# Strassen for two thirds of the first batch element's up projections, and its softmax denominators from one term

## The chip, the cores and the metric

The kernel runs on one core of a Trainium2 chip. A core has five engines that run their own instruction streams: TensorE for matmuls (PE in the profile, its weight loads are PEld), VectorE (DVE), ScalarE (ACT), GpSimd (POOL) and SyncE (SP), which issues most of the DMA transfers here. The metric is the device time of one execution in microseconds; the number given for a kernel is the median of several runs.

## The reference, cut to what matters

Routing attention is followed by a bilinear feed-forward block. Queries and keys are each assigned to the nearest of 16 centroids, and a query sees only the keys of its own cluster.

```python
# attention: batch 4, heads 8, sequence 768, head size 64
mask = q_assign[:, :, :, None] == k_assign[:, :, None, :]
scores = scale * np.matmul(q, k.transpose(0, 1, 3, 2))
scores = np.where(mask, scores, -1000000000.0)
scores = scores - np.max(scores, axis=-1, keepdims=True)
attn = np.exp(scores)
attn = attn / (np.sum(attn, axis=-1, keepdims=True) + 1e-09)
out = np.matmul(attn, v)
# feed-forward: x is (3072, 512), w_a and w_b (512, 1536), w_out (1536, 512)
a = x @ w_a
b = x @ w_b
y = (a * b) @ w_out
```

The weights arrive as 64-bit floats, so the kernel rounds them to 32 bits itself. Everything is computed in float32.

## The kernel before: the parts that the change touches

The program works in **groups**. There are 16 pairs of heads (4 batch elements with 4 pairs each), and 6 groups for each pair, 96 in all. A pair has two halves of 384 queries (`hf`), and a half has six tiles of 128 keys (`j`); a group handles two key tiles. In each group TensorE computes scores of the new tiles (`score`), ScalarE their exponentials (`pt`), and TensorE the weighted sums of values of the tiles before (`weigh`). In the time that is left in a group, pieces of the feed-forward block of the batch element before are run from a queue (`ffn`); a credit of columns per group (`PER_GROUP`) spreads them. What remains in the queue after the last group runs alone.

**Sums over the keys.** The exponentials of a half's tiles are added up elementwise, and a matmul with ones sums the result over the 128 partitions. For the first batch element (`p < HP`, that is pairs 0 to 3) VectorE adds the first five tiles, and the sixth goes into the matmul as a term of its own. For the others both engines share the additions.

```python
    def add_up(u):
        p, hf, j = where(u)
        if j == 0 or j == NJ - 1 and p < HP:
            return
        ...
        for a in range(2):
            many = p >= HP and (a == 1 or j in (2, 4))
            eng = nc.gpsimd if many else nc.vector
            eng.tensor_tensor(out=acc[:, a, :],
                in0=probs[u - 1][:, a, :] if j == 1 else acc[:, a, :],
                in1=probs[u][:, a, :], op=ALU.add)

    def denominators(p, hf):
        ps = apart()
        acc = accs.pop((p, hf))
        terms = [acc]
        if p < HP:
            terms.insert(0, probs[p * UPP + hf * NJ + NJ - 1])
        for n, t in enumerate(terms):
            for a in range(2):
                nc.tensor.matmul(out=ps[a * D:(a + 1) * D, 0:HB], lhsT=ones,
                                 rhs=t[:, a, :], start=(n == 0),
                                 stop=(n == len(terms) - 1))
        ... # ScalarE copies the sums out; VectorE inverts; GpSimd scales xT
```

**Up projections.** A tile of weights has 128 columns; each matmul is issued for 64 of them at a time (`in_halves`). For the first batch element `a` and `b` are computed plainly, 384 tokens (`HB`) at a time, with four chunks of the contraction (`NCH`):

```python
    def ffn_block(b, blk):                       # b = 0 only
        def up(w_sb, f):
            ps = in_turn()                       # one of three banks of PSUM
            for ch in range(NCH):
                in_halves(ps[:, 0:HB], w_sb[:, ch, f * P:(f + 1) * P],
                          xTs[b][:, ch, t0:t0 + HB], ...)
            return ps
        def piece_a(f):                          # ScalarE: ha = a
            ...
        def piece_b(f):                          # VectorE: h = ha * b
            ...
```

For the other three batch elements they go by Strassen's method in Winograd's form (`ffn_ups`): for each pair of weight tiles `i`, `i + N2` and for each of `w_a` and `w_b` there are seven products of two chunks each in place of eight. VectorE makes combinations of the weights (S1 to S4) and of the tokens (T1 to T4), ScalarE copies partial results from PSUM, VectorE adds the others to them, and GpSimd multiplies finished halves of `a` and `b`.

```python
    def combine_x(b):              # queued two pieces before the ups of b
        for c in range(2):
            for out, l, r in ((t3, x22, x12), (x12, x12, x11), (t2, x22, x12)):
                nc.vector.tensor_tensor(out=out, in0=l, in1=r, op=ALU.subtract)
    def ffn_ups(b, h):
        def products(w_sb, i, is_a):
            ...                    # half_1: S1, S2; half_2: S3, S4
            return half_1, half_2, [p1, p2, p6, p5, p7, p3, p4]
        parts = [products(w_sb, i, w_sb is wa_sb) for i in range(NF // 2)
                 for w_sb in (wa_sb, wb_sb)]
```

The down projections (`ffn_downs`) go by Strassen for all four batch elements.

**Rounding the weights.** 36 parts of 128 x 512 weights are loaded and rounded by four VectorE instructions and one addition on GpSimd. ScalarE takes the size of the upper word, and one more VectorE instruction (`flush_w`) sets weights that are too small for a float32 to zero:

```python
            nc.vector.scalar_tensor_tensor(out=w, in0=size, scalar=SMALLEST,
                                           in1=w, op0=ALU.is_ge, op1=ALU.mult)
```

**When things are due.**

```python
    EARLY = BG + 1                           # BG = 24, groups per batch element
    for i in range(8, len(w_parts)):
        due.setdefault(23 + int((i - 8) / 1.5), []).append(i)
    keep_busy(12)                            # transposes of nothing, at the start
    ...
        late = int(g > EARLY)
        if g % 3 == late and 0 < g - late:
            denominators(*divmod(g // 3 - 1, 2))
        ...
        first, second = (4, 1) if g <= EARLY else (5, 3 if g < NG else 2)
```

`long_path` is a second program in the kernel that runs only if a check at the end finds values out of range.

## Time and profile before

| | |
|---|---|
| time, median of 3 | 1047.72 us (1047.59 to 1048.28) |
| span of the profiled execution | 1045.6 us, of 1047.88 us |
| PE busy | 1032.8 us, 7163 instructions |
| DVE, ACT, POOL busy | 657.2, 303.1, 329.9 us |
| stage of batch element 0's attention alone | to about 109 us |
| ups of batch element 0, beside attention of 1 | 109.6 us to about 309 us |
| first product of its downs | 309.4 us |
| feed-forward alone at the end | from about 850 us |

The engines run side by side, so their busy times don't add up. A group of instructions in the profile is named by line, engine, operation, and tiles (output, arrow, inputs), followed by a count, busy time and mean duration. "Idle before" is how long the engine stood still just ahead of these instructions, and the arrow behind it names what ended most of that. The time of PE is best read from the distance between starts, since a matmul's record also covers the time in which it passes through the array.

### The profile page before, as it was taken

How to read it: one execution, taken by the hardware profiler on the slowest of the kernel's cores; microseconds unless marked ns; L12 is line 12 of the kernel's file. 1: busy time of each engine (PE TensorE's matmuls, PEld its weight loads, DVE VectorE, ACT ScalarE, POOL GpSimd, SP SyncE). 2: the span in 40 equal slices, each digit the busy share in tenths (PEclk: the TensorE clock that was granted, in tenths of full speed). 3: DMA queues.
4: the chain of work that ended last, by engine and by line, in shares of the span. 5: the costliest groups of instructions: out<-in, count | busy, mean ns of one | idle time of the engine just before them, and what ended most of it. 6: DMA issues, size and time to landing. Idle time of an engine off the chain costs nothing.

```text
span 1045.6 us, 17833 instructions
## 1 busy us (share of the span) xinstructions
PE 1032.8 (99%) x7163; PEld 502.6 (48%) x7163; DVE 657.2 (63%) x1314; ACT 303.1 (29%) x590; POOL 329.9 (32%) x311
## 2 busy tenths in 40 slices
PE   9999999999999999999999999999999999999997
PEld 5444444444445554444444555444444565444564
DVE  6778877887857447555556746765454845554652
ACT  5665333233322222333323122333232201111100
POOL 1111345455543322343442422443333310211100
PEclk9999999999999999999999999999999999999999
DMA  7334343526120121203020030300000000000001
GB/s 183 87 86 86 85 106 105 125 68 144 63 49 20 40 43 23 38 5 46 4 46 3 24 66 22 49 1 20 1 4 1 11 31 21 1 1 1 2 30 34
DMA packets 120521, 46.48 MB, mean 44 GB/s; under 512 B 106608, under 2 KB 115824, under 8 KB 120432
## 3 DMA queue, kind: packets, MB, share of 16 engines
q1 hardware_dynamic: 120016, 44.85, 18.8%
q8 instruction: 58, 0.95, 0.4%
q10 hardware_dynamic: 416, 0.43, 0.1%
q14 instruction: 31, 0.25, 0.1%
HBM read 37.78 MB, written 6.29 MB: 42 GB/s over the span
## 4 chain that ended last, share of the span: by engine, by line
PE 93%; DVE 4%; issue 1%; POOL 1%; ACT 0%; DMA 0%; DVEq 0%; POOLq 0%
PE m L678 62%; PE s L556 15%; PE O L597 12%; PE s L620 1%; PE s L373 1%; PE m L620 1%; DVE raw L755 1%; PE m L373 0%; POOL xT L652 0%; DVE xT L755 0%; DMA h<-in_q_dram 0%; PE m L354 0%; DVE comb L782 0%; DVE acc L586 0%; DVE acc L647 0%
## 5 line engine op out<-in xcount | busy, mean ns | idle before, releaser
L565 ACT ACTIVATE pt<-s 128x768 f32<-128x768 f32 x192 | 145.3, 808 | 206.5 <-PE s L556 161.7
L586 POOL TENSOR_TENSOR acc<-acc,pt 128x384 f32<-128x384 f32 x144 | 152.6, 1073 | 60.2 <-ACT pt L565 43.0
L597 PE MATMUL O<-pt,v 128*64 128x384 f32 x768 | 145.0, 499 | 0.0
L556 PE MATMUL s<-qkT 64*128 64x384 f32 x768 | 139.7, 482 | 0.0
L821 POOL TENSOR_TENSOR h<-h,ha 128x384 f32<-128x384 f32 x54 | 55.5, 1030 | 258.6 <-DVE ha L815 257.7
L678 PE MATMUL m<-xT,wa_sb 128*64 128x384 f32 x672 | 117.5, 487 | 2.7 <-DVE ha L815 1.0
L678 PE MATMUL m<-xT,wb_sb 128*64 128x384 f32 x672 | 116.9, 487 | 0.0
L815 DVE TENSOR_TENSOR ha<-ha,m 128x384 f32<-128x384 f32 x72 | 39.6, 550 | 98.0 <-PE m L678 75.4
L586 DVE TENSOR_TENSOR acc<-acc,pt 128x384 f32<-128x384 f32 x96 | 74.5, 802 | 36.6 <-POOL acc L586 35.5
L815 DVE TENSOR_TENSOR h<-h,m 128x384 f32<-128x384 f32 x72 | 39.5, 548 | 80.7 <-PE m L678 53.8
L812 ACT COPY h<-m 128x384 f32<-128x384 f32 x72 | 34.5, 479 | 184.9 <-PE m L678 184.9
L597 PEld LDWEIGHTS O<-pt,v 128*64 128x64 f32 x768 | 46.6, 136 | 85.8 <-issue 80.1
L678 PE MATMUL m<-wo_sb,h 128*64 128x256 f32 x768 | 86.7, 379 | 0.0
L556 PEld LDWEIGHTS s<-qkT 64*128 64x128 f32 x768 | 70.5, 187 | 31.3 <-issue 0.2
L678 PEld LDWEIGHTS m<-xT,wa_sb 128*64 128x64 f32 x672 | 48.7, 137 | 63.4 <-issue 53.3
L678 PE MATMUL m<-raw 128*64 128x384 f32 x432 | 78.9, 486 | 0.0
L652 POOL TENSOR_TENSOR xT<-xT,acc 128x384 f32<-128x384 f32 x32 | 32.8, 1026 | 144.9 <-DVE acc L647 144.6
L678 PEld LDWEIGHTS m<-xT,wb_sb 128*64 128x64 f32 x672 | 49.0, 137 | 60.1 <-issue 56.2
L678 PEld LDWEIGHTS m<-wo_sb,h 128*64 128x64 f32 x768 | 54.9, 137 | 31.1 <-issue 5.0
L678 PE MATMUL m<-xT,h 128*64 128x256 f32 x576 | 64.5, 379 | 0.0
L678 PE MATMUL m<-xT,size 128*64 128x384 f32 x288 | 52.7, 487 | 0.0
L678 PEld LDWEIGHTS m<-xT,h 128*64 128x64 f32 x576 | 41.3, 137 | 22.3 <-issue 2.3
(169 smaller groups left out, 1302.0 us busy)
## 6 DMA issues: line engine op xcount, KB each, us to landing
raw<-in_moe_w_a_dram SPq DMA_DIRECT2D x12, 512.0 KB, 3.8
raw<-in_moe_w_b_dram SPq DMA_DIRECT2D x12, 512.0 KB, 3.6
raw<-in_moe_w_out_dram SPq DMA_DIRECT2D x12, 512.0 KB, 3.7
qk<-in_q_dram SPq DMA_DIRECT2D x48, 96.0 KB, 3.1
qk<-in_k_dram SPq DMA_DIRECT2D x48, 96.0 KB, 3.6
v<-in_v_dram SPq DMA_DIRECT2D x24, 192.0 KB, 3.8
out_dram<-rest SPq DMA_DIRECT2D x24, 128.0 KB, 1.7
v<-in_v_dram SPq DMA_DIRECT2D x4, 384.0 KB, 4.5
```

Of the source, the lines that this page charges most:

```text
L373: nc.tensor.matmul(out=ps[32 * kq:32 * kq + 32, 0:HB], lhsT=cTb[:, hp, :], rhs=qkTs[p][:, kq * HB:(kq + 1) * HB], start=True, stop=True)
L556: nc.tensor.matmul(out=s[:, a, 0:HB], lhsT=Ts[p][r, S + j * P:S + (j + 1) * P], rhs=Ts[p][r, hf * HB:(hf + 1) * HB], start=start, stop=not ...
L565: nc.scalar.activation(out=pt, in_=s[:, :, 0:HB], func=AF.Exp, scale=SCALE)
L586: eng.tensor_tensor(out=acc[:, a, :], in0=probs[u - 1][:, a, :] if j == 1 else acc[:, a, :], in1=probs[u][:, a, :], op=ALU.add)
L597: nc.tensor.matmul(out=O_of[0][a * D:(a + 1) * D, 0:HB], lhsT=vs[p][:, a, j, :], rhs=probs[u][:, a, :], start=(j == 0), stop=(j == NJ - 1))
L620: nc.tensor.matmul(out=ps[a * D:(a + 1) * D, 0:HB], lhsT=ones, rhs=t[:, a, :], start=(n == 0), stop=(n == len(terms) - 1))
L652: nc.gpsimd.tensor_tensor(out=x, in0=x, in1=den, op=ALU.mult)
L678: nc.tensor.matmul(out=ps[half], lhsT=lhsT[:, half], rhs=rhs, **kw)
L755: nc.vector.tensor_tensor(out=out, in0=l, in1=r, op=ALU.subtract)
L812: nc.scalar.copy(out=box[name], in_=box["X"][:, 0:HB])
L815: nc.vector.tensor_tensor(out=box[name], in0=box[name], in1=box[bank][:, 0:HB], op=ALU.add)
L821: nc.gpsimd.tensor_tensor(out=to, in0=to, in1=box[name], op=ALU.mult)
```

## The change

The change does five things, with the aim of taking matmuls off TensorE and work off VectorE.

1. Of the first batch element's up projections, the weight tiles 0 to 7 (of 12) go by Strassen, in four pairs (0, 2), (1, 3), (4, 6), (5, 7), since the weights of the first tiles are rounded first; tiles 8 to 11 stay plain. Combinations of tokens are made early, and kept in rows of `h` that the plain tiles fill later.
2. In the first batch element the sixth key tile is added up by GpSimd, and the matmul with ones has one term. It comes a group later, and so does the normalization. In the other batch elements GpSimd takes tiles 4 and 5 in place of 2 and 4.
3. The instruction that zeroes small weights is gone. ScalarE looks for a weight that is too small (`see_w`), and if there is one, `long_path` zeroes such weights and computes everything again.
4. The feed-forward block of the first batch element becomes ready as a whole, no longer in two halves, and parts 8 to 35 of the weights come up to three groups later.
5. Smaller moves: the combinations of tokens for batch elements 1 to 3 come in two pieces, fewer empty transposes at the start, and other engines for the first copies.

```diff
 # cuts are marked by ...
     def add_up(u):
-        if j == 0 or j == NJ - 1 and p < HP:
+        if j == 0:
             return
-            many = p >= HP and (a == 1 or j in (2, 4))
+            many = a == 1 or j > 3 if p >= HP else j == NJ - 1
     def denominators(p, hf):
-        terms = [acc]
-        if p < HP:
-            terms.insert(0, probs[p * UPP + hf * NJ + NJ - 1])
-        for n, t in enumerate(terms):
-            for a in range(2):
-                nc.tensor.matmul(... rhs=t[:, a, :], start=(n == 0), ...)
+        for a in range(2):
+            nc.tensor.matmul(... rhs=acc[:, a, :], start=True, stop=True)
...
-        late = int(g > EARLY)
-        if g % 3 == late and 0 < g - late:
+        if g % 3 == 1 and g > 1:
             denominators(*divmod(g // 3 - 1, 2))
-        first, second = 4, 1          # for g <= EARLY
+        first, second = (5, 2) if g <= EARLY else (5, 3 if g < NG else 2)
-    EARLY = BG + 1
+    EARLY = BG + 2
...
     def ffn_ups(b, h):
+        N2, firsts = (NF // 2, range(NF // 2)) if b else (2, (0, 1, 4, 5))
-        parts = [products(...) for i in range(NF // 2) for w_sb in (wa_sb, wb_sb)]
+        parts = [products(...) for i in firsts for w_sb in (wa_sb, wb_sb)]
     def ffn_ready(p, hf):
-        elif hf == 0:
-            blocks[0] = ffn_block(0, 0)
-            ffn.extend(blocks[0][0][0:8])
...
+            for name in ("T3", "T2", "T4"):
+                combination_x(0, name, 1)
+            ffn.extend(ups_first + plain_ups(0, h, range(NF - 4, NF)))
+    def early_steps():
+        return {HP * GPP - 10: both(begin, T("T1", 0)), HP * GPP - 8: T("T1", 1),
+                HP * GPP - 3: T("T3", 0), HP * GPP - 2: T("T2", 0),
+                HP * GPP - 1: T("T4", 0),
+                HP * GPP: lambda: [f() for f in combinations[0:2]],
+                HP * GPP + 1: lambda: combinations[2]()}
...
-            ffn.insert(len(ffn) - FREE_ROOM, (0, lambda: combine_x(b)))
+            for c in range(2):
+                ffn.insert(len(ffn) - FREE_ROOM + c, (0, lambda c=c: combine_x(b, c)))
...
     def round_w(i):
-        size = sizep.tile([P, WN], FP32, name="size")
-        nc.scalar.activation(out=size, in_=halves(FP32)[:, :, 1], func=AF.Abs)
-    def flush_w():
-            nc.vector.scalar_tensor_tensor(out=w, in0=size, scalar=SMALLEST,
-                                           in1=w, op0=ALU.is_ge, op1=ALU.mult)
+    def see_w():
+        while unseen:
+            i, upper = unseen.pop()
+            nc.scalar.activation(out=size, in_=upper, func=AF.Abs)
+            nc.scalar.activation(out=size, in_=size, func=AF.Relu, scale=-STEEP,
+                                 bias=edge[:, 0:1], accum_out=stat[:, n:n + 1])
+            load_w(i + 2)
...
         if p == HP:
-            return [[lambda: across(0), lambda: across(1)], [sims_across],
-                    assign[:2], assign[2:], [one_hot, one_hot_across], []]
+            return [[lambda: across(0), lambda: across(1)],
+                    [sims_across] + assign[:2], assign[2:] + [one_hot],
+                    [one_hot_across], [], []]
-            ready[1] = both(lambda: prep_sim(p), lambda: load_v(p), ready[1])
+            ready[1] = both(lambda: prep_sim(p), lambda: load_v(p), steps[1][0],
+                            lambda: todo.extend(steps[1][1:]))
...
-        due.setdefault(23 + int((i - 8) / 1.5), []).append(i)
+        due.setdefault(26 + int((i - 8) / 1.45), []).append(i)
-        (UP + DOWN * 7 / 8, BG + 5.8), ...
+        (UP * 11 / 12 + DOWN * 7 / 8, BG + 1.8), ...
-    keep_busy(12)
+    keep_busy(5)
     prep_transpose(0, 0)
+    keep_busy(2)
-        if p == 0 and i == 2:
-            nc.vector.tensor_copy(out=dst[:, 0:256], in_=ps[:, 0:256])
-            nc.scalar.copy(out=dst[:, 256:], in_=ps[:, 256:])
-        elif p == 0 and i != 1 or p == 1 and i == 2:
+        if p < 2 and i == 2:
             nc.vector.tensor_copy(out=dst, in_=ps)
```

## The prediction

> **What bounds the kernel now.** I read the page from the top: busy times, then the chain that ended last, then the waits of PE alone, and only then single stretches of the trace.
>
> ```profile
> PE 1032.8 (99%) x7163; PEld 502.6 (48%) x7163; DVE 657.2 (63%) x1314; ACT 303.1 (29%) x590; POOL 329.9 (32%) x311
> PE 93%; DVE 4%; issue 1%; POOL 1%; ACT 0%; DMA 0%; DVEq 0%; POOLq 0%
> PE m L678 62%; PE s L556 15%; PE O L597 12%; PE s L620 1%; PE s L373 1%; PE m L620 1%; DVE raw L755 1%; PE m L373 0%; POOL xT L652 0%; DVE xT L755 0%; DMA h<-in_q_dram 0%; PE m L354 0%; DVE comb L782 0%; DVE acc L586 0%; DVE acc L647 0%
> ```
>
> The first line says that TensorE is nearly always busy and no other engine is above 63%. The second and third say that the chain which sets the end is PE's own work, 62% of it the feed-forward matmuls (L678). A busy PE can still be a slow PE, so I looked at what it waits for. This is the list of waits of PE, whole but for its smallest entries:
>
> ```profile
> PE O L1053 <- DVE ones L80: 1.1, 1, 1.1
> PE m L678 <- DVE ha L815: 1.0, 2, 0.5
> PE s L556 <- DVE sim L481: 1.0, 1, 1.0
> PE m L678 <- POOL xT L652: 0.9, 1, 0.9
> PE m L678 <- DVE rest L939: 0.9, 2, 0.4
> PE m L373 <- DVE cTb L325: 0.6, 1, 0.6
> PE s L620 <- DVE acc L586: 0.5, 1, 0.5
> ```
>
> Columns: total us, times, longest. Added up, PE waits 6 us in a kernel of 1047.72. So time can come almost only from PE work that is not issued, and can go almost only into new waits of PE.
>
> The chain in order of time gives the price of PE work (start, us, what, records):
>
> ```profile
> 152.71 1.44 PE O L597 x8
> 154.16 5.16 PE m L678 x32
> 159.31 1.72 PE s L556 x12
> 161.04 1.44 PE O L597 x8
> ```
>
> 32 records of a feed-forward matmul over 384 tokens take 5.16 us, so one takes 161.2 ns. The groups list 672 such records of xT with wa_sb, while the program issues 336 matmuls of that kind (192 plain ones, 144 of Strassen's products): each matmul in the code leaves two records and costs **322.5 ns**. The mean of 487 ns that the list prints is the passage through the array, three records deep, and is not the price.
>
> **What the Trainium skill says.** (1) "Perfetto Trace Analysis", section "Identifying the Most-Contended Engine": matmul busy share is a poor measure, since pipelined matmuls overlap. The trace agrees (487 ns printed against 161.2 ns of pitch), and that is why I price by pitch. (2) "SBUF — State Buffer", section "SBUF: two separate sides": a VectorE instruction with two SBUF inputs and a GpSimd one exclude each other, each for a whole instruction. The trace fits: VectorE's adds of `acc` and `pt` take 802 ns in the mean, one that begins at 399.58 takes 550, and one at 500.62 takes 1160 while GpSimd adds. Work given to GpSimd therefore slows VectorE. (3) "ScalarE: Activation LUTs", section "Table sets: the hidden batching unit": relu and abs are in every table set. So the new Relu should load no table; before there are two loads, both at the start, of 1283 ns. Were it otherwise, 36 parts would bring up to 72 loads. (4) "TensorE: Matmul & The Clock Gate", section "What's actually happening": the clock falls after an idle window of about 3.4 us. Fewer empty transposes leave gaps of under 1 us at the start, which is far from that; the granted clock in the page never drops below 0.9.
>
> **The change part by part.**
>
> *Up projections.* Plain, the first batch element takes 2 weights x 12 tiles x 2 token blocks x 4 chunks x 2 halves = 384 matmuls. After it, 4 pairs x 2 weights x 7 products x 4 = 224 by Strassen and 4 tiles x 2 blocks x 2 weights x 8 = 128 plain, 352 in all. 32 fewer x 322.5 ns = **10.3 us**, all of it on PE in a stage that PE bounds.
>
> *Denominators.* 8 halves of the first batch element each lose the term of the sixth tile: 2 matmuls each, 16 x 322.5 ns = **5.2 us**. Is PE the bound there too, with no feed-forward work to fill in? Yes: from 14.3 to 98.7 us, the stage of attention alone, it is busy for 83.85 of 84.40 us, and in its timeline a group's matmuls follow on the last one's without a gap. GpSimd pays 16 additions of about 1.07 us; it is busy for only 15.56 us of that stage.
>
> *Start.* The first empty transposes run from 3.84 to 5.94 us, while the copies of the queries that the first real transposes need were done at 5.05. With 5 in place of 12 they can start some 0.5 us earlier. Also, now ScalarE and VectorE each evacuate a part of the last transposes one after the other (7.88 and 8.34 us); VectorE alone will do it at once. The chain through VectorE's cTb (0.6 us wait above) stays. I count **0.5 us**.
>
> *VectorE.* Two stretches show how much room it has (stretch, its length, then busy us and instructions of PE, PEld, DVE, ACT, POOL):
>
> ```profile
> 124.00:310.00 186.00, 185.05 (x1163) 81.41 (x1161) 141.89 (x220) 63.19 (x118) 93.94 (x81) 1.00 0.39 97
> 395.00:565.00 170.00, 169.07 (x1064) 72.70 (x1062) 98.07 (x214) 52.57 (x102) 64.40 (x63) 1.00 0.16 25
> ```
>
> The first is plain ups of batch element 0 together with the rounding: VectorE 76%. The second is Strassen's ups of batch element 1: VectorE 58%. In the first the change takes away the zeroing (27 instructions in this stretch, 28.8 us) and 16 of 24 multiplications at 546 ns (8.7 us). It adds 64 weight combinations at a mean of 376 ns (24.1 us: eight per product set, 288 of them in the kernel before take 108 us), 32 additions at 550 ns and 4 multiplications at 540 ns (19.8 us). Net +6.4 us, in a stage shorter by 10.3 us but for new waits: 148 of some 177 us, **84%**. That is high, but off PE's path as long as the three PSUM banks come free in time. Something helps: in this stretch VectorE stands still for 17.0 us in `acc` additions that wait for GpSimd's (tiles 2 and 4 go to GpSimd in turn with VectorE's 3 and 5). With VectorE doing 1 to 3 and GpSimd 4 and 5, this ping-pong ends.
>
> *ScalarE.* 36 times an Abs (as before, 683 ns) and a Relu with its accumulator read (683 + about 200 ns, from the rows of such reads): +32 us on an engine with 29%. Hidden.
>
> *Waits that move.* The 0.95 us wait of scores for the copy of `sim` at 137.61 should go, as that transpose now follows its matmul directly:
>
> ```profile
> 136.32 0.34 PE L556 MATMUL s<-ohT 64*128 64x384 bf16 x2
> 137.61 0.34 PE L556 MATMUL s<-ohT 64*128 64x384 bf16 x2 [0.95 <-DVE sim L481]
> ```
>
> At 396.4 and 645.3 PE waits 0.43 us each for a bank (the L939 entry), behind six combinations of tokens in a row on VectorE, 5.7 us; cut in two pieces, most of it goes. Together **1.7 us** off. The 0.88 us wait at the first feed-forward piece, for normalized xT, changes form: now the first product that needs the last half is p6, the third, behind three more VectorE subtractions. I leave it as it is.
>
> *New waits.* Strassen beside rounding at 84% VectorE, and the start of it in groups 26 to 28, where normalization, combinations and rounding meet: I allow **1.5 us**. This is a judgement: the ups of batch element 1 show 0.43 and 0.50 us of PE waits, at 58% VectorE; here VectorE is fuller, so I take half as much again.
>
> Sum: -10.3 - 5.2 - 0.5 - 1.7 + 1.5 = -16.2, so 1047.7 - 16.2 = **1031.5 us**, 1.5% less.
>
> **The rivals.**
>
> *VectorE becomes the bound of the first batch element's feed-forward.* For it: 84% busy, in-order work, bursts of four rounding instructions (2.2 us) ahead of an addition that frees a bank, and 12 more GpSimd multiplications that lock the shared port. Against it: at 76%, with 17 us of blocking besides, it costs PE 0.1 us in 20 us. If it wins, 5 to 10 us of the 15.5 come back: 1036 to 1041.
>
> *The denominators wait for GpSimd.* The sum now ends with two GpSimd additions in place of a VectorE one. For it: PE stands in order behind it, 8 times. Against it: the matmul is a group later (3.5 us here at least), GpSimd is nearly idle, 2 x 1.07 us fit. If 0.5 us were lost each time, 4 us come back: 1035.
>
> *The feed-forward starts later and PE starves.* It becomes ready after group 26 and not after 22. But no stretch before has PE idle, so its pieces do not fill holes; they only move to later groups, and what is left runs at the end. It costs nothing unless the bare groups 22 to 26 are bound by VectorE, which is busy for 21.39 of the 25.30 us from 98.7 to 124. I give this 1 to 2 us, inside the range.
>
> *Nothing is gained, for the time was hidden.* PE's 99% and its 6 us of waits speak against it.
>
> **Range and chances.** Both large terms are counts times a measured pitch, so they can hardly be off by 1 us. The uncertain part is waits: at best none are new and the start gains 1 us, 1028.5; at worst VectorE gives back 5 us, 1036.5. Faster by over 2% would need 1026.8 or less, 5 us more than the sum, and there is hardly that much waiting to remove. Slower by over 2% would need 37 us of new waits, such as table loads or the second program running.
>
> **What would show it.** PE records: 7163 - 64 - 32 - 5 = 7062 (an empty transpose leaves one record). In the chain 32 records still take 5.16 us. The L620 groups on `pt` are gone and PE waits for `acc` stay under 1 us in all. VectorE is at 80 to 87% in the ups of batch element 0, its wait for GpSimd's `acc` falls from 35.5 us to under 10. Two table loads. The prediction is wrong if PE's waits add up to more than 10 us, if the pitch changes, or if the first stage of attention shortens by less than 4 us.

## The result, and the profile after

The changed kernel takes **1061.89 us** (median of 4 runs, 1061.72 to 1062.65), the one before 1047.70. The ratio is 1.0136, with a 95% interval of 1.0118 to 1.0153: 1.4% slower, where 1.5% faster had been foreseen. The profiled execution spans 1059.9 us (before 1045.6).

From the page of the kernel after, the busy times and the chain by engine:

```profile
PE 1024.4 (97%) x7062; PEld 493.9 (47%) x7062; DVE 699.2 (66%) x1370; ACT 336.7 (32%) x674; POOL 368.1 (35%) x339
PE 82%; DVE 13%; issue 2%; ACT 1%; POOL 1%; DMA 0%; DVEq 0%; POOLq 0%
```

PE has 7062 records, exactly the number foreseen, so the matmuls did go. But PE is at 97% and no longer 99%, and its share of the chain fell from 93% to 82%, while VectorE's rose from 4% to 13%. VectorE is busy for 42.0 us more and GpSimd for 38.2 us more. The list of PE's waits says where it stands (total us, times, longest):

```profile
PE m L680 <- DVE h L835: 8.2, 5, 3.0
PE m L680 <- ACT h L831: 7.3, 1, 7.3
PE s L563 <- ACT pt L572: 2.9, 8, 0.6
PE m L623 <- POOL acc L594: 2.7, 7, 0.4
PE O L605 <- ACT xT L615: 2.2, 3, 1.2
PE m L680 <- DVE ha L835: 1.9, 2, 1.2
```

The whole list adds up to some 29 us, and before to some 7. Three of these rows (L835 and L831, 17.4 us) are Strassen products that wait for a bank of PSUM or for an operand. The other three (7.8 us) belong to attention: scores wait for the exponentials' buffers, the denominators for the sums, the values for the copies of their results.

Four stretches of the kernel after: attention alone, the groups of the hand-over, its worst piece, and the ups of batch element 0. The columns are the stretch, its length, busy us and instructions of PE, PEld, DVE, ACT and POOL, then the granted clock, the DMA share and GB/s:

```profile
13.50:101.00 87.50, 82.33 (x546) 36.62 (x547) 77.88 (x121) 58.32 (x108) 30.02 (x24) 1.00 0.35 80
101.00:131.00 30.00, 26.75 (x158) 10.61 (x160) 29.45 (x52) 16.28 (x30) 14.28 (x12) 1.00 0.47 95
131.00:150.00 19.00, 10.88 (x60) 4.11 (x58) 17.41 (x26) 4.75 (x12) 11.64 (x10) 0.82 0.31 88
150.00:320.00 170.00, 160.41 (x990) 67.55 (x988) 143.75 (x238) 78.37 (x160) 89.07 (x77) 0.99 0.37 91
```

The last three of the kernel before, for comparison:

```profile
101.00:131.00 30.00, 28.66 (x174) 13.93 (x170) 25.22 (x46) 11.44 (x23) 8.24 (x7) 1.00 0.27 76
131.00:150.00 19.00, 18.05 (x116) 7.48 (x114) 12.86 (x22) 5.86 (x11) 7.72 (x7) 1.00 0.53 116
150.00:320.00 170.00, 170.00 (x1092) 74.78 (x1089) 131.67 (x204) 57.69 (x107) 85.95 (x75) 1.00 0.36 89
```

The reader is to see VectorE's column beside PE's. From 101 to 131 us VectorE is busy for 29.45 of 30 us: there it has no room at all. From 131 to 150 us it has 17.41 of 19 us, and PE does 10.88 us of work where it did 18.05. From 150 to 320 us PE, which had never stood still, misses 9.6 us, with VectorE at 85%.

**The largest hole** lies in the third stretch. In the timeline of PE of the kernel after (start, us, instruction; in brackets the idle time before it and what ended it):

```profile
130.95 2.75 PE L680 MATMUL m<-xT,wa_sb 128*64 128x384 f32 x16
141.03 2.83 PE L680 MATMUL m<-h,pair 128*64 128x384 f32 x8 [7.33 <-ACT h L831]
```

The bracket names ScalarE, but ScalarE had itself stood still for 7.90 us before, waiting for VectorE's `acc` of line 649. So one looks at VectorE over the same time:

```profile
131.30 1.65 DVE L283 SCALAR_TENSOR_TENSOR wb_sb<-raw,wb_sb 128x512 int32<-128x512 int32 x1
...
134.70 1.26 DVE L508 TENSOR_TENSOR sim<-sim,mx 128x384 f32<-128x384 f32 x1
...
139.61 1.33 DVE L767 TENSOR_TENSOR h<-xT 128x384 f32<-128x384 f32 x1 [1.11 <-POOL xT L654]
140.87 2.62 DVE L767 TENSOR_TENSOR h<-xT,h 128x384 f32<-128x384 f32 x2
```

VectorE never rests but for 1.11 us. It works through, in order, the rounding of a part, the cluster assignment of a pair, a normalization, and only then the token combinations (L767) that the products need. And several instructions take twice what they should: L283 takes 0.69 us elsewhere and 1.65 here, an addition over 384 columns 0.55 us elsewhere and 1.31 to 1.33 here. What runs beside the last two, on GpSimd:

```profile
139.54 4.81 POOL L594 TENSOR_TENSOR acc<-acc,pt 128x384 f32<-128x384 f32 x4
```

Those are sums of exponentials of pair 4, tiles 4 and 5. GpSimd had seven such additions for each half of this pair before as well; the change only dealt them in another order. Beside the first two lines (131.30 and 134.70) stand GpSimd's additions of the rounding, at 131.01 and 134.28 us. The instructions of the two engines hold each other up. The same pattern stands in attention alone, here beside sums that the change did give to GpSimd. A part of VectorE's and of GpSimd's timeline there, in the kernel after:

```profile
54.73 2.62 DVE L594 TENSOR_TENSOR acc<-pt 128x384 f32<-128x384 f32 x2
...
54.35 2.58 POOL L594 TENSOR_TENSOR acc<-acc,pt 128x384 f32<-128x384 f32 x2
```

Before, the same two VectorE additions took 1.02 us in all (at 53.60 us), with GpSimd idle beside them. In the groups, the row of these first additions reads before:

```profile
L586 DVE TENSOR_TENSOR acc<-pt 128x384 f32<-128x384 f32 x40 | 22.4, 575 | 16.1 <-POOL xT L652 11.5 <-ACT pt L565 4.6
```

and after, followed by that of the further additions:

```profile
L594 DVE TENSOR_TENSOR acc<-pt 128x384 f32<-128x384 f32 x40 | 32.6, 831 | 11.7 <-POOL xT L654 11.7
L594 DVE TENSOR_TENSOR acc<-acc,pt 128x384 f32<-128x384 f32 x96 | 70.2, 757 | 1.3
```

40 instructions as before, but 831 ns and not 575 each. The second row has lost its wait for GpSimd (idle 36.6 us before, 1.3 us after), as was foreseen.

**VectorE's account over the whole kernel.** I added up the rows of VectorE's groups by kind of instruction, before and after. The changed counts, at the mean durations of before, give +5.2 us: 36 zeroing instructions less (-35.0), 64 weight combinations more (+24.1), the rest, mostly additions and multiplications, +16.1. The changed means give **+42.5 us**: the instructions are the same, but they take longer. The rows' sum is 5.7 us more than the busy time shows (47.7 against 42.0), as neighbouring records overlap a little. **What they run beside.** Every VectorE instruction that took over 0.1 us longer than the short ones of its shape overlaps an instruction of GpSimd. There are 129 of them before and 180 after, and together they are 92.8 and 131.6 us longer. Counted by the GpSimd instruction that each overlaps most, this grew from 60.1 to 72.0 us beside the sums of exponentials, from 17.6 to 27.9 us beside the multiplications, and from 3.2 us (4 instructions) to 20.8 us (23) beside the additions of the rounding, though these are 36 in both kernels. Before, mostly transposes, reciprocals and instructions that read PSUM ran beside them, and those are not slowed. So the largest part of the growth is not from work that GpSimd was given: other VectorE instructions have come to stand beside work that it had. In return, the 36.6 us in which VectorE had stood still for GpSimd's sums are gone.

That is the first theory, **V**: VectorE, slowed by GpSimd's instructions beside it, is late in groups and stretches where PE depends on it.

### The profile page after: what moved, and what is told of

Read it like the earlier page. It is cut to its first block, busy times and chain, and to the rows that moved or that the text cites. A ratio compares the mean times of both kernels' runs of the same rounds, so it can differ in the third digit from the quotient of the medians.

```text
span 1059.9 us, 17911 instructions
## 1 busy us (share of the span) xinstructions
PE 1024.4 (97%) x7062; PEld 493.9 (47%) x7062; DVE 699.2 (66%) x1370; ACT 336.7 (32%) x674; POOL 368.1 (35%) x339
## 4 chain that ended last, share of the span: by engine, by line
PE 82%; DVE 13%; issue 2%; ACT 1%; POOL 1%; DMA 0%; DVEq 0%; POOLq 0%
PE m L680 56%; PE s L563 12%; PE O L605 10%; DVE acc L594 2%; PE s L623 1%; DVE pair L799 1%; PE s L378 1%; DVE wb_sb L283 1%; DVE rest L287 1%; DVE xT L927 1%; DVE rest L290 1%; DVE comb L799 1%; DVE h L767 1%; ACT pt L572 0%; POOL acc L594 0%
## 5 line engine op out<-in xcount | busy, mean ns | idle before, releaser
L594 POOL TENSOR_TENSOR acc<-acc,pt 128x384 f32<-128x384 f32 x160 | 177.4, 1128 | 46.3 <-ACT pt L572 37.4
L841 POOL TENSOR_TENSOR h<-h,ha 128x384 f32<-128x384 f32 x66 | 68.7, 1044 | 251.7 <-DVE ha L835 250.5
L835 DVE TENSOR_TENSOR ha<-ha,m 128x384 f32<-128x384 f32 x88 | 48.1, 550 | 109.2 <-PE m L680 86.2
L831 ACT COPY h<-m 128x384 f32<-128x384 f32 x88 | 42.1, 478 | 210.9 <-PE m L680 207.5
L835 DVE TENSOR_TENSOR h<-h,m 128x384 f32<-128x384 f32 x88 | 47.8, 545 | 75.3 <-PE m L680 48.5
L680 PE MATMUL m<-xT,wb_sb 128*64 128x384 f32 x480 | 84.6, 492 | 4.4 <-DVE h L835 4.4
L680 PE MATMUL m<-xT,wa_sb 128*64 128x384 f32 x480 | 83.4, 487 | 1.9 <-DVE ha L835 1.9
L831 ACT COPY ha<-m 128x384 f32<-128x384 f32 x66 | 31.5, 478 | 106.2 <-PE m L680 106.2
L680 PEld LDWEIGHTS m<-xT,wb_sb 128*64 128x64 f32 x480 | 34.2, 138 | 49.0 <-issue 36.9
L680 PEld LDWEIGHTS m<-xT,wa_sb 128*64 128x64 f32 x480 | 34.1, 137 | 45.3 <-issue 38.1
```

The costliest lines, as they stand in the source:

```text
L594: eng.tensor_tensor(out=acc[:, a, :], in0=probs[u - 1][:, a, :] if j == 1 else acc[:, a, :], in1=probs[u][:, a, :], op=ALU.add)
L680: nc.tensor.matmul(out=ps[half], lhsT=lhsT[:, half], rhs=rhs, **kw)
L831: nc.scalar.copy(out=box[name], in_=box["X"][:, 0:HB])
L835: nc.vector.tensor_tensor(out=box[name], in0=box[name], in1=box[bank][:, 0:HB], op=ALU.add)
L841: nc.gpsimd.tensor_tensor(out=to, in0=to, in1=box[name], op=ALU.mult)
```

## The experiments

The expectations were written before each run. Letters in them name the theories of that set; V is the one above. The kernel before measured 1047.98 to 1048.16 us beside these runs; each ratio is taken against it, with its 95% interval. The edits are cut; `...` marks what is left out.

### First set: one part of the change at a time

**The sums alone**, on the kernel before.

```diff
-        if j == 0 or j == NJ - 1 and p < HP:
+        if j == 0:
-            many = p >= HP and (a == 1 or j in (2, 4))
+            many = a == 1 or j > 3 if p >= HP else j == NJ - 1
-        ... # the second term of denominators
-        late = int(g > EARLY)
-        if g % 3 == late and 0 < g - late:
+        if g % 3 == 1 and g > 1:
-    EARLY = BG + 1
+    EARLY = BG + 2
...
```

> The kernel before with the change of the sums alone (sixth key tile by GpSimd, one-term denominators a group later, GpSimd's tiles 4 and 5 in the other batch elements; the feed-forward keeps its early pieces). Theory S (several engines' queues): GpSimd's additions lock the port against VectorE, exponentials wait for buffers that these additions hold, and the 5.2 us of PE work come back as waits before group 22: 1046 to 1050 us. Rival T (only Strassen costs time, the sums work as counted): 1042.5 us, with group 22 starting 4.5 us earlier than before.

1055.07 us, 1.0062 (1.0045 to 1.0078), above both expectations. The 16 matmuls are gone, and yet it is 7 us slower. PE's waits:

```profile
PE s L556 <- ACT size L294: 5.3, 1, 5.3
PE m L618 <- POOL acc L586: 2.3, 6, 0.4
PE s L556 <- DMA ohT<-oh: 2.0, 1, 2.0
```

Scores wait for 7.3 us in the groups of the hand-over, 2.0 of it for a transfer of the one-hot assignments of pair 4. The whole change prepares that pair a group earlier, so this kernel lacked something that the change has (with that preparation, in the first run of the third set, both of these waits go). It shows that the hand-over has no slack, not what the sums cost by themselves.

**The late start alone**: the feed-forward of batch element 0 becomes ready as a whole.

```diff
-        if hp < HP - 1:
+        if hp < HP - 1 or hf == 0:
             return
-            blocks[0] = ffn_block(0, 0)        # and the first pieces after half 0
+            # both blocks are made after half 1
...
```

> The kernel before with its feed-forward block of batch element 0 made ready as a whole after the second half of pair 3, no early pieces; all ups still plain, no PE work removed. Theory S: the early pieces were what covered VectorE's backlog in groups 23 to 27, so PE waits 5 to 9 us there: 1053 to 1057 us. Rival T (the 7.3 us wait at the start of the feed-forward comes from Strassen's combinations): 1047.5 to 1050 us.

1056.14 us, 1.0073 (1.0057 to 1.009). The number fits the theory of a starving start, but its waits do not: 5.5 us are again for the transfer of the one-hots (twice, 3.3 at the longest) and 1.7 us for a transpose of queries and keys. As with the sums, the change's earlier preparation of pair 4 is missing; no run adds it to the late start. A number that fits is not yet a cause.

**The zeroing alone**: it leaves VectorE, and ScalarE looks for small weights.

```diff
-            nc.vector.scalar_tensor_tensor(out=w, in0=size, scalar=SMALLEST,
-                                           in1=w, op0=ALU.is_ge, op1=ALU.mult)
+            nc.scalar.activation(out=size, in_=upper, func=AF.Abs)
+            nc.scalar.activation(out=size, in_=size, func=AF.Relu, ...)
...
```

> The kernel before with the zeroing of small weights taken from VectorE and the look for them given to ScalarE, nothing else. VectorE loses 35 us of work, PE none. Theory S: PE waits little in the kernel before, so little can be gained: 1045 to 1047.5 us. Rival A (ScalarE's second instruction delays exponentials and the copies out of PSUM): 1049 us or more.

1048.57 us, 1.0005 (0.9996 to 1.0014), between the two expectations. 35 us less on VectorE bring nothing where VectorE is not in PE's way. In the first groups it loses 3.0 us (scores wait for exponentials, behind ScalarE's looks of 680 + 722 + 187 ns a part) and regains them later.

**The whole change but for Strassen**: all ups of batch element 0 plain.

```diff
-            ffn.extend(ups_first + plain_ups(0, h, range(NF - 4, NF)))
+            ffn.extend(plain_ups(0, h, range(NF)))
...
```

> The changed kernel with all ups of batch element 0 plain, everything else kept (sums, no zeroing, late start, rounding due later). PE has 10.3 us more work than in the changed kernel. Theory S: the waits of 3.0, 2.2, 1.8 us and others in Strassen's products between 190 and 260 us go, about 11 us with the lower clock behind them; the wait of 7.3 us at the start shrinks but stays by half or more: 1056 to 1062 us. Rival T (Strassen alone costs the time): 1042 to 1044 us.

1048.68 us, 1.0006 (0.9997 to 1.0015), between the two expectations. This is the run that cuts the loss in two. It keeps the sums, the late start, the look and the preparation, and PE does not wait at the hand-over. So all that together nets nothing: the 5.2 us of saved denominators are given back in waits of attention (exponentials 2.9, sums 2.3, copies 1.7 us). Strassen's part alone costs 1061.89 - 1048.68 = **13.2 us**, though it takes 10.3 us of matmuls away. Some 23.5 us of waiting arise where it runs beside the rounding.

### Second set: what of Strassen's part

**Shorter rounding**: the changed kernel, but the weights' parts 8 to 35 are cut to 20 bits, which leaves out two VectorE instructions (1.12 us) and one GpSimd addition (1.3 us) for each part. The weights are coarser than the reference's.

```diff
+        if i >= 8:
+            unseen.append((i, halves(FP32)[:, :, 1]))
+            return
         rest = wtp.tile([P, WN], FP32, name="rest")
```

> The changed kernel, but weight parts 8 to 35 are cut to 20 bits of mantissa and not rounded: per part two VectorE instructions (1.12 us) and one GpSimd addition (1.3 us) less, 31 and 36 us in all, from group 26 on. No PE work changes. Theory V (in the stage where Strassen of batch element 0 and rounding lie together, VectorE with the port it shares with GpSimd can't keep up): most waits between 140 and 260 us go, and the wait at the start of the ups shrinks by some 3 us: 1046 to 1053 us. Rival D (waits come from the order of dependent products, ScalarE's copies and banks, not from load): 1058 to 1062 us.

1044.16 us, 0.9963 (0.9949 to 0.9977): 17.7 us faster than the changed kernel, with the same matmuls. The stretch of the ups:

```profile
150.00:320.00 170.00, 170.00 (x1086) 74.47 (x1084) 109.72 (x204) 82.95 (x169) 65.03 (x60) 1.00 0.38 95
```

VectorE fell from 143.75 to 109.72 us and PE is without a gap. The hole at the hand-over shrank from 7.3 to 3.2 us. This is better than the theory's own range, and it shows that the work beside PE, not the matmuls' order, made the loss. It does not yet separate VectorE from GpSimd.

**Is it ScalarE's queue?** The hole names ScalarE's copy, which stands behind the check of the inverses in that queue. Here that check is put off by a group.

```diff
-        check_inverses()
+        if g != EARLY + 1:
+            check_inverses()
```

> The changed kernel with ScalarE's check of the inverses in group 27 put off by one group, so that ScalarE's copy of the first product does not stand behind VectorE's normalization. Rival Q (ScalarE's queue makes the wait of 7.3 us): it goes, 1054 to 1056 us. Theory V: PE gets one more product done and then waits for T2 of the last half, which stands in VectorE's queue: 1059 to 1062 us.

1062.76 us, 1.014 (1.0123 to 1.0157): nothing gained, as theory V had it, just above its range. The wait only changed its name:

```profile
PE m L680 <- DVE h L767: 7.9, 1, 7.9
```

Now it is the token combinations in VectorE's queue. ScalarE was the messenger.

**The old sums in the changed kernel**: two terms for batch element 0, the feed-forward a group earlier.

```diff
-        if j == 0:
+        if j == 0 or j == NJ - 1 and p < HP:
-    EARLY = BG + 2
+    EARLY = BG + 1
+        ... # the second term of denominators is back
...
```

> The changed kernel with the sums of batch element 0 as before (VectorE alone, two terms, a group earlier, so that the feed-forward starts a group earlier too). PE has 5.2 us more work. If the sums save what was counted: 1067 us. If they give it all back as waits, as the first runs say: 1060 to 1063 us. If they cost more than they save beside Strassen, through GpSimd's port: under 1059 us.

1067.71 us, 1.0189 (1.0172 to 1.0206): 5.8 us more than the changed kernel, close to the 5.2 us of the matmuls that came back. But the start came a group earlier too, and VectorE's waits moved (7.6 and 6.7 us for its `ha` and `h`), so two things are mixed. It says only that the new sums were not what made the changed kernel slow.

**One third by Strassen**: two pairs in place of four, after four plain tiles.

```diff
-        N2, firsts = (NF // 2, range(NF // 2)) if b else (2, (0, 1, 4, 5))
+        N2, firsts = (NF // 2, range(NF // 2)) if b else (2, (4, 5))
...
```

> The changed kernel with one third of the ups by Strassen (tiles 4 to 7), tiles 0 to 3 plain and first, so that the combinations of the last half are made while plain products run. PE has 5.2 us more work than in the changed kernel and 5.2 less than with all ups plain (1048.7 us). Theory V with the start as the largest single place: 1044 to 1049 us. Rival: each Strassen product beside rounding costs waits alike, whatever starts, about 12 us for half of them: 1054 us or more.

1049.2 us, 1.001 (1.0003 to 1.0017), just above theory V's range. The hole at the hand-over is gone, as the first plain tiles need no combinations. But two products still wait, 2.5 us up to 223.55 and 1.5 us up to 234.91, beside the rounding. 16 matmuls fewer than with plain ups (5.2 us), and no faster.

### Third set: VectorE's load or GpSimd's additions

**The sums with pair 4 prepared early**, on the kernel before.

```diff
-            return [[...], [sims_across], assign[:2], assign[2:], [one_hot, one_hot_across], []]
+            return [[...], [sims_across] + assign[:2], assign[2:] + [one_hot],
+                    [one_hot_across], [], []]
...
```

> The kernel before with the change of the sums and the earlier preparation of pair 4, nothing else: the run with the sums alone had 7.3 us of waits in group 24 for pair 4's one-hot rows, which the changed kernel doesn't have. If those were all that is wrong: 1042.5 us, the 5.2 us as counted. Theory S (the sums give back most of their gain in the attention stage, by GpSimd's additions that hold VectorE up): 1046 to 1049 us.

1056.85 us, 1.008 (1.0063 to 1.0097); neither expectation held. The wait for one-hots is gone, and one of the same size has come:

```profile
PE m L678 <- POOL xT L652: 6.3, 1, 6.3
```

The first feed-forward piece now waits for normalized tokens, whose inverse stands behind the rounding in VectorE's queue. In the kernel before, the rounding of parts 8 and up begins in group 23, and the last normalization now comes a group later, into the middle of it.

**The same with the sixth tile on VectorE** in place of GpSimd.

```diff
-            many = a == 1 or j > 3 if p >= HP else j == NJ - 1
+            many = p >= HP and (a == 1 or j > 3)
```

> As the run with sums and preparation, but VectorE adds the sixth key tile of batch element 0 itself: 16 additions of 550 ns more on VectorE (8.8 us), 16 fewer on GpSimd. Theory L (an addition on GpSimd stops a VectorE instruction with two SBUF inputs for its own length, so that handing it over frees nothing): within 1.5 us of the run with sums and preparation, on either side. Rival (GpSimd's work is free for VectorE): slower than that run by 3 us or more.

1054.61 us, 1.0065 (1.0048 to 1.0082): 2.2 us faster than with GpSimd, more than the 1.5 us foreseen, although VectorE does 16 additions more. VectorE's busy time even fell, from 685.4 to 682.2 us. Group 22 starts 3.96 us before its old time, and not 2.10. An addition handed to GpSimd is not free: it holds up VectorE's.

**The rounding's addition on VectorE** in the changed kernel.

```diff
-        nc.gpsimd.tensor_tensor(out=w, in0=w, in1=rest, op=ALU.add)
+        nc.vector.tensor_tensor(out=w, in0=w, in1=rest, op=ALU.add)
```

> The changed kernel with the addition of the rounding on VectorE and not on GpSimd: 36 additions over 512 columns, 680 ns each on VectorE (24.5 us more), 1300 ns each on GpSimd (47 us less). Theory L: GpSimd's additions cost VectorE up to their own 1300 ns, so the change is even or faster: 1052 to 1062 us. Rival O (VectorE is overloaded by its own instructions, the port matters little): 19 us more work in the overloaded stage, 1066 to 1078 us.

1060.35 us, 1.0116 (1.0099 to 1.0133), 1.5 us faster. VectorE has 36 instructions more, which by themselves would take some 24 us, and its busy time went only from 699.2 to 701.0 us, as GpSimd's fell from 368.1 to 322.0. The blocking fell by about as much as work was added. So it is VectorE's whole time, own work and blocking together, that counts; it does not help to take the blocking away if the work comes in its place.

**One term for the second halves only**, with the splits and the start of the change.

```diff
-        if j == 0 or j == NJ - 1 and p < HP:
+        if j == 0 or j == NJ - 1 and p < HP and hf == 0:
...
```

> A version made from what the runs say: the kernel before with the one-term sums for the second half of each pair alone (VectorE's assignment of clusters comes in the other half), the earlier preparation of pair 4, the combinations of tokens in two pieces and the shorter start; zeroing, plain ups of batch element 0 and early pieces as before. PE work: 4 halves x 0.645 = 2.6 us less. Theory S: 2.6 + 0.4 + about 1 us of waits gained, 1043 to 1045.5 us. If any sum with GpSimd gives its gain back: 1046 to 1048 us.

1056.86 us, 1.0079 (1.0062 to 1.0096), far above both expectations. The sums themselves now end in time-critical places:

```profile
PE m L619 <- DVE acc L585: 6.5, 5, 3.6
```

### Fourth set: VectorE's load without Strassen

**Useless work on VectorE**: the kernel before, with two more multiplications after each of the 24 of the plain ups, whose results nobody uses.

```diff
+            for _ in range(2):
+                nc.vector.tensor_tensor(out=box["a"], in0=box["a"],
+                                        in1=box["h"][:, f, :], op=ALU.mult)
```

> The kernel before with two more VectorE multiplications of 128x384, both inputs in SBUF and the result not used, behind each of the 24 plain second pieces (48 in all, 550 ns clear and about 1000 ns beside GpSimd: 26 to 48 us). PE work, its order and the banks stay. VectorE goes from 76% to 90 or 97% in the ups of batch element 0. Theory V (load alone does it): 6 to 25 us of new waits, 1053 to 1072 us. Rival D (only Strassen's dependent products wait): 1047.5 to 1049.5 us.

1076.59 us, 1.0269 (1.0253 to 1.0285), somewhat above the top of what was expected. From the groups:

```profile
L712 DVE TENSOR_TENSOR ha<-ha,h 128x384 f32<-128x384 f32 x48 | 42.7, 890 | 1.7
```

and the largest of PE's waits in the same kernel:

```profile
PE s L373 <- DVE qkT L477: 11.9, 2, 5.9
PE s L556 <- ACT acc L625: 3.8, 2, 1.9
```

42.7 us of VectorE work cost 28.6 us of time: **0.67 us for each us**, with the same 7163 records on PE, no Strassen, no change to the sums. From 124 to 310 us VectorE is busy for 156.83 of 186 us, 84%, the very share that the prediction had called high but harmless, and PE is busy for 165.97. So VectorE's load alone makes PE wait, without the change. PE's listed waits grew by some 20 of the 28.6 us; the granted clock was also at half for 17.1 us. A high share is not enough by itself, though: from 150 to 180 us VectorE is busy for 28.14 of 30 us and PE for all 30, from 180 to 210 us VectorE for 24.66 and PE for 23.84. What counts is whether PE soon needs something that stands behind the queue, here the transposed queries and keys of the next pair (11.9 us in two waits).

**The sums once more on the kernel before**, with VectorE, pair 4 early, the rounding from group 25 on and the combinations in two pieces.

```diff
-        due.setdefault(23 + int((i - 8) / 1.5), []).append(i)
+        due.setdefault(25 + int((i - 8) / 1.6), []).append(i)
...
```

> The kernel before with one-term sums whose sixth tile VectorE adds, the earlier preparation of pair 4, weight parts 8 to 35 rounded from group 25 on in place of 23, and the combinations of tokens in two pieces; zeroing, plain ups of batch element 0 and its early pieces as before. PE work 5.2 us less. Theory S (rounding in front of the normalization made the wait of 3.5 to 6.5 us at the first plain pieces in the runs with the sums): 1041 to 1045 us. Rival (the later normalization by itself makes PE wait, whatever else VectorE does): 1048 us or more.

1049.35 us, 1.0014 (1.0007 to 1.0021), in the rival's range and not in the theory's. Its waits are 2.2 us for normalized tokens, 2.2 us for copies and 1.8 us for one-hots. In none of these forms did the shorter denominators pay on the kernel before; each time waits in attention and at the hand-over gave them back.

### Fifth set: what would pay

Three kernels cut the weights to 24 bits with a single VectorE instruction (a shift and an or), which takes one VectorE instruction and GpSimd's addition out of each part. They leave out the rounding to nearest: the last bit is cut off.

```diff
-        nc.vector.tensor_scalar(out=rest.bitcast(INT32), ... op0=ALU.bitwise_and)
-        nc.vector.scalar_tensor_tensor(out=rest, in0=lo, scalar=2.0 ** -52, ...)
-        nc.gpsimd.tensor_tensor(out=w, in0=w, in1=rest, op=ALU.add)
+        nc.vector.scalar_tensor_tensor(
+            out=w.bitcast(UINT32), in0=lo, scalar=29, in1=w.bitcast(UINT32),
+            op0=ALU.logical_shift_right, op1=ALU.bitwise_or)
```

**On the changed kernel:**

> The changed kernel with weights cut to the 24 bits of a float32 by one VectorE instruction (shift and or, 690 ns) in place of two (430 and 690 ns) and GpSimd's addition (1300 ns): the last bit is not rounded to nearest. VectorE's own instructions are 36 x 0.43 = 15 us fewer, GpSimd's 47 us fewer. If only VectorE's own time counts: about 0.67 us of time for each us in the stage of ups (12 us there), 1053 to 1056 us. If GpSimd's additions count as VectorE time too (theory L): 1042 to 1050 us.

1045.57 us, 0.9976 (0.9967 to 0.9986): 16.3 us less than the changed kernel. VectorE falls from 699.2 to 653.7 us. Only some 15 us of that are the instructions left out (36 of about 0.43 us). No other was left out, so the other 30 us are instructions that became shorter, above all where GpSimd's additions beside them went.

**On the kernel before, as a control:**

> The kernel before with weights cut in the same way, as a control. It has 6 us of PE waits, little of it by rounding: 1045.5 to 1047.5 us by both theories.

1045.19 us, 0.9973 (0.9962 to 0.9984): 2.8 us, just under what was expected. The same work taken away is worth six times as much after the change as before it. VectorE's busy time fell by 16.7 us here, hardly more than the instructions left out: before the change, the rounding's additions on GpSimd held up almost nothing. But it also means that with the cut the change still brings nothing (1045.57 against 1045.19): its saved matmuls only pay for its remaining waits, of which the hand-over's is 4.7 us.

**On one third by Strassen, with the sixth tile on VectorE:**

> The kernel with one third by Strassen (1049.2 us), with weights cut in the same way and the sixth key tile added by VectorE. Theory L: 4.5 us of waits beside Strassen and 2 us in the attention stage go, 1041 to 1045 us. Otherwise 1046 to 1049 us.

1040.75 us, 0.9933 (0.9915 to 0.9951), just under what was expected, and the fastest of all: 4.4 us below the control. Its busy times:

```profile
PE 1021.9 (98%) x7094; PEld 495.8 (48%) x7094; DVE 633.7 (61%) x1308; ACT 333.0 (32%) x668; POOL 290.4 (28%) x281
```

32 more records than the changed kernel, but VectorE has 65.5 us less, and PE's largest wait is 2.2 us in all. It beats both kernels, at the price of the last bit of the weights.

## Why the prediction was wrong

**Right: the work on PE.** 7062 records, as counted, and the pitch did not change (32 records in 5.16 us at 276.58 us). The 15.5 us of matmuls did leave PE. So did the 0.95 us wait for the copy of `sim` and the two of 0.43 us at the combinations (they end at 397.31 and 646.25 us, somewhat later than the prediction placed them); but those two went in the run with the sums alone as well, which does not cut the combinations in two. The start gained 0.35 us (group 0 at 13.53 and not 13.88 us), where 0.5 were counted. There are two table loads as before. VectorE's wait for GpSimd's `acc` went.

**Wrong: the step "148 of some 177 us, 84%. That is high, but off PE's path", and with it the "new waits" of 1.5 us.** The listed waits of PE went from some 7 to some 29 us. The distances between its starts beyond the longest usual pitch of each shape, which also hold the lower clock, went from 8.7 to 35.7 us by my count. -15.5 us of work and +27.0 us of these make +11.5, most of the measured +14.2. Two things failed in it:

1. *The size of VectorE's load.* The prediction's net of +6.4 us for the stage is near the rows' +5.2 for the whole kernel, in part by luck: it counted 27 of the 36 zeroings, and not the 8 more combinations of tokens (some 6 us). It left out what it had itself quoted under the Trainium skill, "SBUF — State Buffer", section "SBUF: two separate sides": VectorE instructions with two SBUF inputs and GpSimd's exclude each other. The trace agrees (0.55 us clear, 1.31 to 1.33 us beside GpSimd). It even said that work given to GpSimd slows VectorE, and then priced the 16 new additions as hidden, because GpSimd was "nearly idle". It named 12 new multiplications on GpSimd too, but only as an argument of a rival. That VectorE's instructions would come to stand beside other GpSimd work than before, above all the rounding's additions, is in no term of it. VectorE's longer instructions came to +42.5 us, eight times the counted term.
2. *What a share of 84% means.* The share itself came in: 168.84 of 197.00 us from 131 to 328 us, 86%, where 80 to 87% had been foreseen, though with more work in a longer stage. But it is a mean. While Strassen's products run, from 150 to 262 us, VectorE is busy for 102.07 of 112 us (91%) and PE for 102.42; over the plain ones behind them, to 328 us, VectorE is at 75% and PE without a gap. With the shorter rounding VectorE is busy for 78.34 of the same 112 us, and PE for all of them. The run with useless work had 84% and lost 0.67 us for each us added. Over the whole kernel VectorE is at 66%, while the groups of the hand-over reach 98% (29.45 of 30 us) and PE waits for what stands behind them.

**Wrong: "It costs nothing unless the bare groups 22 to 26 are bound by VectorE".** They were. The prediction had put 21.39 of 25.30 us beside it and given it 1 to 2 us. The hand-over collects a normalization, the rounding, the next pair's assignment and the token combinations, and made the one hole of 7.33 us, in which PE's granted clock also fell: the mean is 0.82 from 131 to 150 us. The Trainium skill's "TensorE: Matmul & The Clock Gate", section "What's actually happening", says that the clock falls after an idle window of about 3.4 us. The trace agrees: PE's last record before the hole ends at 133.70 us, and the granted clock is at half from 137.5 to 144.3 us. The prediction had quoted this, and had thought only of the gaps at the start.

**Wrong: the first stage of attention shortens by 5 us.** Group 22 starts at 104.34 us, before at 103.72. By then PE has issued 16 matmuls of denominators fewer (14 terms are gone, and the seventh half's own two come later; 5.2 us), and with the start (0.4) this should have brought it to 98.2. Some 6 us were lost, most of it to waits for exponentials, sums and copies. The sums' chain is the cause in part: with GpSimd out of it the same sums were 2.2 us faster. For the rest, ScalarE's looks are likely (the run with the zeroing alone lost 3.0 us by group 21), but no run had the changed kernel without them.

**The rivals and ScalarE.** The rival of VectorE as the bound won, but at several times its 5 to 10 us. That of denominators waiting for GpSimd was right in kind and size: 2.7 us in 7 waits, where up to 4 had been allowed. ScalarE's added work was sized right (+32 counted, 303.1 to 336.7 us measured). 1061.9 us is 25 us above the range's upper end, which had allowed VectorE 5 us.

The prediction's own signs, waits of PE above 10 us and a first stage that shortens by less than 4 us, both came in.

**Open.** How the 7.33 us divide between rounding, assignment and token combinations: shorter rounding left 3.2 us of it, and with plain tiles first it was gone, but no run took the assignment away. Whether the shorter denominators can pay at all on the kernel before: six microseconds of new waits at the hand-over hid the answer each time. What the lower clock costs was not measured by a run. An estimate from the trace: it was at half from 137.5 to 144.3 and from 216.0 to 219.4 us, and PE worked for 6.7 us of that, so about 3.3 us were lost; eight records that take 1.46 us elsewhere took 2.83 us at 141.03 and 2.46 us at 215.59.

## What to carry to other kernels

When one engine is at 99%, matmuls taken off it are worth their pitch only if the engines that feed it and empty its banks have room in the same groups; look at stretches of 20 to 30 us around each hand-over, not at a stage's mean, and at what PE needs from behind a full queue. Price an instruction given to GpSimd twice: for itself, and for the VectorE instruction with two operands in SBUF that it may hold up. And when VectorE's work moves in time, look at which GpSimd instructions it will run beside, even if their number stays. And when the first experiments remove a part and a new wait of the same size comes in its place, suspect one full queue behind all of them.

## What was not expected of the hardware

The size of the blocking, from the records of VectorE before and after: an elementwise instruction over 384 columns with two tensors in SBUF as its inputs takes 549 and 551 ns in the mean when no GpSimd instruction overlaps it, and 1030 and 1044 ns when one does. With one input in PSUM it takes 551 and 548 ns, and 543 ns in both kernels beside GpSimd, so it isn't touched. Over 128 columns it is 283 and 281 ns against 745 and 699. The mean loss is 0.42 to 0.49 us in both, so a short instruction loses the larger share. This fits Strassen's small weight combinations, 128 columns each, which went from a mean of 376 ns (288 of them) to 398 (352 of them). A rounding step with a single tensor as its input grew as well: L280 over 512 columns takes 0.42 us at 130.85 us and 1.22 us at 143.41 us, beside a GpSimd addition.
